# A fixed order for the first forty steps of each engine, first units in halves, filling products on TensorE

## The chip, the cores and the metric

The kernel runs on one core of a Trainium2 chip. The metric is the device time of one execution in microseconds; the kernel before takes 868.29 us (median of 3 runs, 868.08 to 869.13). Engines: PE (TensorE), ACT (ScalarE), DVE (VectorE), POOL (GpSimd), SP (issues the DMAs).

## The reference

q, k and v have 8 batches, 8 heads, 576 positions, 64 dims. Attention is within chunks of 64 positions; its output, heads laid side by side, is a matrix x of 4608 tokens by 512, which goes through a feed-forward part with weights 512 x 2048 and 2048 x 512 (given as 8-byte numbers).

```
scores = scale * q_c @ k_c.T              # per chunk of 64, scale = 1/8
attn   = exp(scores - max) / (sum + 1e-9)
x      = (attn @ v_c), heads side by side # [4608, 512]
h      = x @ w_in
g      = h * 1 / (1 + exp(-1.702 * h))
out    = g @ w_out                        # [4608, 512] float32
```

## The kernel before

Tokens are taken in 36 tiles of 128; four tiles are a block, and there are 9 blocks. The hidden dimension is cut into 16 parts of 128. One unit g (144 in all) is one block and one part: h_g is 12 matmuls of 512 columns into a PSUM bank (three products of high and low parts for each of four pieces of the model dimension, lines 634 to 636), ACT applies gelu (line 655) and copies the high part g_h (656), DVE subtracts for the low part g_l (660), and o_g_t, for each tile t of the block, adds three matmuls to that tile's output bank po_t (669 to 671). For unit 0 alone h comes in two halves of 256 columns, but in one bank, and gelu follows both.

Each of the 16 weight blocks w_j (w_in's and w_out's part j) is loaded as 8-byte words (plan_w: raw_j, two DMAs of 512 KB) and made into a high and a low part: wsc and wlow on ACT (lines 172, 176), a shift with an or on DVE (181, 182), an addition (188, called wj), wh on ACT (193), and the difference on DVE (196), after which w_j is ready. They are needed once, in the order of the units of block 0, and stay.

The first four tiles, u = 0 to 3, go through plan_first: loads of q, k, v (256 KB each), transposes of q and k on PE (266), copies to SBUF on ACT and DVE (273, 277, 279), scores on PE (289), max and subtraction on DVE (294, 295), exp on ACT (298), sum and reciprocal on DVE (302 to 305), the product with the reciprocal on POOL (308), transposes on PE (313), a copy on ACT (320), the product with v on PE (329), and x's high part on ACT (339) and low part on DVE (342). The later tiles go in pairs (plan_pair), pair 4 and pair 6 with transposes on PE (412, 480), beside block 0's units.

The order is set by class Plan: each step has an engine, a cost, a rank, the events that it needs and the buffers that it takes and gives. emit() plays the steps through with these costs and handover times, gives each free engine its ready step of the lowest rank, and writes the instructions in that order. Each engine then runs its instructions in program order and waits for what a step needs. Two buffers exist for h (bank pair hp) and for g, one output bank per tile.

Of the kernel before, what the change touches and what calls it, by code (L numbers as in the profile page):

```python
# [20 lines left out]

class Plan:
# [6 lines left out]
    HANDOVER = {None: 0.0, PE: 0.2, ACT: 0.2, DVE: 0.15, POOL: 0.15, DMA: 2.0}  # L29
    TABLE_LOAD = 1.3  # L30

    def __init__(self, buffers):
        self.free = dict(buffers)
        self.steps = []

# [3 lines left out]
    def emit(self):  # L39
# [13 lines left out]
        table, now, left = None, 0.0, len(self.steps)  # L53
        order = []
        while left:
            for e, heap in ready.items():
                while heap and busy[e] <= now + 1e-9:
                    skipped, pick = [], None
                    while heap:
                        rank, i = heapq.heappop(heap)  # L60
                        take = self.steps[i][6]
                        if all(self.free[b] >= take.count(b) for b in take):
# [15 lines left out]
                    post(now + cost + (self.HANDOVER[e] if e == DMA else 0), 0, give)  # L78
                    post(now + cost + self.HANDOVER[e], 1, make)
            assert at or not left, sorted((s[2], s[5]) for h in ready.values() for s in [self.steps[i] for _, i in h])[:9]  # L80
            now = at[0][0] if at else now
            while at and at[0][0] <= now + 1e-9:
                _, _, kind, what = heapq.heappop(at)
                if kind == 0:
                    for b in what:
                        self.free[b] += 1
                else:
                    for i in users.pop(what, ()):
# [10 lines left out]
def tile_chunk_attention_ffn(  # L99
# [14 lines left out]
    P = 128  # L114
# [22 lines left out]
    make_identity(nc, ident)  # L137

# [10 lines left out]
    def slot_user(j):  # L149

        return divmod(NF - 1 - j, 2)

    def plan_w(j):
# [23 lines left out]

        def high():
            hf, hi, li, lu = words()
            w_tmp[j] = tmp = more.tile([P, 1024], I32, tag="wtmp", name=f"wtmp_{j}")  # L180
            nc.vector.tensor_scalar(tmp, hi, 3, None, op0=ALU.logical_shift_left)
            nc.vector.scalar_tensor_tensor(
                tmp, hi, -(2**31), tmp, op0=ALU.bitwise_and, op1=ALU.bitwise_or
# [19 lines left out]
        u, kind = slot_user(j)  # L203
        need = [f"{('s', 'xp')[kind]}_{u}"] if u < TB else []
        e = lambda n: f"{n}_{j}"
        plan.add(DMA, 1.6, rank - 5.5, lambda: load(0), need=need, make=e("rawi"), take=[f"w{j}"])
        plan.add(DMA, 1.6, rank - 5.5, lambda: load(1), need=[e("rawi")], make=e("raw"))
        plan.add(ACT, 1.1, rank, scale, need=[e("raw")], make=e("wsc"))
        plan.add(ACT, 1.1, rank, low, need=[e("wsc")], make=e("wlow"))
        plan.add(DVE, 1.95, rank, high, need=[e("wsc")], make=e("whigh"), take=["tmp"])  # L210
        plan.add(DVE, 1.25, rank, join, need=[e("whigh"), e("wlow")], make=e("wj"))
        plan.add(ACT, 1.05, rank - 3.5, part_h, need=[e("wj")], make=e("wh"))
        plan.add(DVE, 1.25, rank - 2, part_l, need=[e("wh")], make=e("w"), give=["tmp"])
# [27 lines left out]
    def plan_first(u):  # L241
# [29 lines left out]

        def t_q():
            nc.scalar.activation(st["tr"][:, 0], st["ps"][0], AF.Copy)

        def t_k():
            if k_act:
                nc.scalar.activation(st["tr"][:, 1], st["ps"][1], AF.Copy)
            else:
                nc.vector.tensor_copy(st["tr"][:, 1], st["ps"][1])

        def s_pe():
            t = st["tr"]
            st["s"] = sc = ps_o.tile([P, NP, 2, CH], F32, tag=f"po{u % 2}", name=f"s_{u}")
# [7 lines left out]
        def s_max():  # L291
            sc = st["s"]
            m = two.tile([P, NP, 2], F32, tag="m", name=f"m_{u}")
            nc.vector.tensor_reduce(m, sc, axis=AX.X, op=ALU.max)
            nc.vector.tensor_tensor(st["e"], sc, bc(m), op=ALU.subtract)
# [11 lines left out]
        def s_norm():  # L307
            nc.gpsimd.tensor_tensor(st["e"], st["e"], bc(st["r"]), op=ALU.mult)  # L308

        def e_pe():  # L310
            st["ps"] = ps = ps_o.tile([P, NP, 2, CH], F32, tag=f"po{2 + u % 2}", name=f"eTp_{u}")
# [10 lines left out]
        def x_pe():  # L322
            va, et = st["v"], st["et"]
            ps = ps_a.tile([P, 2, 2, NP, CH], F32, tag="att", name=f"x_{u}")
            for n in range(NP):
                for h in range(2):
                    for c in range(2):
                        r = slice(64 * c, 64 * c + 64)
                        nc.tensor.matmul(
                            ps[64 * h : 64 * h + 64, c, 0, n, :],  # L330
                            va[r, 2 * n + h, :],
                            et[r, n, h, :],
                            start=True,
                            stop=True,
                        )
            st["x"] = ps[:, :, 0].rearrange("p c n i -> p n c i")

        def x_hi():
            nc.scalar.activation(x_part(x_h, u), st["x"], AF.Copy)

        def x_lo():
            nc.vector.tensor_tensor(x_part(x_l, u), st["x"], x_part(x_h, u).bitcast(F32), op=ALU.subtract)

        rank = u - 95
        plan.add(DMA, 2.0, u - 103, load_qk, make=ev("rows"), take=[slot(0)])
        plan.add(DMA, 1.0, u - 102.5, load_v, make=ev("v"), take=[slot(1)])
        plan.add(PE, 0.95, rank, t_pe, need=[ev("rows")], make=ev("tp"), take=["hp", "hp"])
        plan.add(ACT, 0.6, rank, t_q, need=[ev("tp")], make=ev("tq"), give=["hp"])
        plan.add(ACT if k_act else DVE, 0.68, rank, t_k, need=[ev("tp")], make=ev("tk"), give=["hp"])
        plan.add(  # L350
            PE, 1.2, rank + 0.6, s_pe, need=[ev("tq"), ev("tk"), ev("v")], make=ev("s"),
            take=[f"po{u % 2}"], give=[slot(0)],
        )
        plan.add(DVE, 1.37, rank + 0.6, s_max, need=[ev("s")], make=ev("m"), give=[f"po{u % 2}"])
        plan.add(ACT, 0.63, rank + 0.6, s_exp, need=[ev("m")], make=ev("ex"), table="exp")
        plan.add(DVE, 1.1, rank + 0.6, s_sum, need=[ev("ex")], make=ev("z"))
        plan.add(POOL, 1.07, rank + 0.6, s_norm, need=[ev("z")], make=ev("n"))
        plan.add(PE, 0.5, rank + 1.7, e_pe, need=[ev("n")], make=ev("ep"), take=[f"po{2 + u % 2}"])
        plan.add(ACT, 0.6, rank + 1.7, e_act, need=[ev("ep")], make=ev("et"), give=[f"po{2 + u % 2}"])
        plan.add(  # L360
            PE, 0.75, rank + 1.5, x_pe, need=[ev("et"), ev("v"), "xa_0"], make=ev("xp"),
            take=["att", "att"], give=[slot(1)],
        )
        plan.add(ACT, 0.6, rank + 1.5, x_hi, need=[ev("xp")], make=ev("xh"))
        plan.add(DVE, 0.69, rank + 1.5, x_lo, need=[ev("xh")], make=ev("xl"), give=["att", "att"])

# [4 lines left out]
    def plan_pair(u):  # L371
# [162 lines left out]
        if pe:  # L534
            for t in range(2):
# [9 lines left out]
                plan.add(ACT, 0.6, rank, lambda t=t: t_q(t), need=[ev(f"tp{t}")], make=ev(f"tq{t}"), give=["att"])  # L545
                plan.add(DVE, 0.68, rank, lambda t=t: t_k(t), need=[ev(f"tp{t}")], make=ev(f"tk{t}"), give=["att"])
# [225 lines left out]
```

## Time and profile before

| what | value |
|---|---|
| median of 3 runs | 868.29 us |
| the profiled execution | 868.24 us, its span 866.5 us |
| PE busy | 849.3 us (98%), 5882 matmul instructions |
| DVE busy, ACT busy, POOL busy | 392.3 us (45%), 319.1 us (37%), 32.3 us (4%) |
| mean granted clock of TensorE | 0.993 |

Read it with care: the shares are means over the whole span. The span in 40 slices has PE at 7 and 6 tenths at its two ends and 9 tenths between, DVE at 9 tenths in slices 3 and 4 and ACT at 9 in slices 2 to 4. Busy times of matmuls overlap one another.

### The profile page before, as it was taken

The numbers are of one execution on the slowest core, as the hardware profiler recorded it, in microseconds if no ns is written. First come the engines' busy times: TensorE is split into PE (matmuls) and PEld (weight loads), VectorE is DVE, ScalarE is ACT, GpSimd is POOL, SyncE is SP. The second block draws the span as 40 slices with busy tenths as digits, with TensorE's granted clock in tenths as the row PEclk, the third lists the DMA queues.
The fourth block names the chain that finished last, engine by engine and source line by source line (L and its number), as shares of the span: only waits on it lengthen the run. The fifth ranks groups of instructions, "written<-read, shape, count | busy, mean of one in ns | idle before, by whom it ended". The sixth has DMA issues, their size and how long they took to land.

```text
span 866.5 us, 14153 instructions
## 1 busy us (share of the span) xinstructions
PE 849.3 (98%) x5882; PEld 703.0 (81%) x5882; DVE 392.3 (45%) x511; ACT 319.1 (37%) x459; POOL 32.3 (4%) x24
## 2 busy tenths in 40 slices
PE   7699999999999999999999999999999999999998
PEld 5588888888888888888888888888888888888886
DVE  5899985353534252616253444445343524121111
ACT  3999652332424242324242423223241424222221
POOL 1000000000000000000000000000000000000000
PEclk9799999999999999999999999999999999999999
DMA  9997243234313022402231232113101010010001
GB/s 236 319 300 212 45 74 80 52 56 73 92 25 49 22 47 57 72 2 48 74 58 18 41 75 51 31 38 85 25 1 26 37 35 3 1 45 5 1 0 49
DMA packets 194592, 55.47 MB, mean 64 GB/s; under 512 B 179680, under 2 KB 187872, under 8 KB 194528
## 3 DMA queue, kind: packets, MB, share of 16 engines
q1 hardware_dynamic: 194528, 54.57, 27.3%
q8 instruction: 46, 0.75, 0.4%
q14 instruction: 18, 0.15, 0.1%
HBM read 45.09 MB, written 9.44 MB: 63 GB/s over the span
## 4 chain that ended last, share of the span: by engine, by line
PE 95%; SPq 2%; DMA 1%; DVE 1%; ACT 1%; issue 1%; POOL 0%; DVEq 0%; POOLq 0%; ACTq 0%
PE po L669 16%; PE po L670 15%; PE po L671 15%; PE hp L634 15%; PE hp L635 15%; PE hp L636 15%; PE s L445 2%; PE x L510 2%; SPq L231 1%; DMA raw<-in_moe_w_out_dram 1%; PE qkTp L412 0%; ACT raw L172 0%; POOL first_b L308 0%; PE eTp L480 0%; SPq L163 0%
## 5 line engine op out<-in xcount | busy, mean ns | idle before, releaser
L660 DVE TENSOR_TENSOR g_l<-hp,g_h 128x512 fp32r<-128x512 f32 x144 | 99.5, 691 | 351.2 <-ACT g_h L656 350.1
L669 PE MATMUL po<-w,g_l 128*128 128x512 f32 x576 | 226.4, 393 | 0.1
L671 PE MATMUL po<-w,g_h 128*128 128x512 f32 x576 | 224.3, 389 | 0.0
L670 PE MATMUL po<-w,g_h 128*128 128x512 f32 x576 | 224.2, 389 | 0.0
L634 PE MATMUL hp<-x_l,w 128*128 128x512 f32 x572 | 223.2, 390 | 0.0
L636 PE MATMUL hp<-x_h,w 128*128 128x512 f32 x572 | 222.7, 389 | 0.0
L635 PE MATMUL hp<-x_h,w 128*128 128x512 f32 x572 | 222.6, 389 | 0.0
L655 ACT ACTIVATE hp<-hp 128x512 f32<-128x512 f32 x144 | 83.9, 583 | 305.3 <-PE hp L636 269.6
L656 ACT ACTIVATE g_h<-hp 128x512 fp32r<-128x512 f32 x144 | 86.1, 598 | 141.3 <-PE po L671 139.6
L669 PEld LDWEIGHTS po<-w,g_l 128*128 128x128 f32 x576 | 108.1, 188 | 23.9 <-DVE g_l L660 1.0
L671 PEld LDWEIGHTS po<-w,g_h 128*128 128x128 f32 x576 | 108.1, 188 | 22.7
L670 PEld LDWEIGHTS po<-w,g_h 128*128 128x128 f32 x576 | 108.1, 188 | 21.8
L636 PEld LDWEIGHTS hp<-x_h,w 128*128 128x128 f32 x572 | 107.4, 188 | 22.8 <-DVE w L196 0.4
L634 PEld LDWEIGHTS hp<-x_l,w 128*128 128x128 f32 x572 | 107.4, 188 | 22.4 <-DVE g_l L660 0.2
L635 PEld LDWEIGHTS hp<-x_h,w 128*128 128x128 f32 x572 | 107.4, 188 | 22.0
L493 DVE STREAM_TRANSPOSE eT<-e 32x512 f32<-32x512 f32 x112 | 78.7, 703 | 29.6 <-POOL e L473 27.8
L473 POOL TENSOR_TENSOR e<-e,r 128x1024 f32<-128x1024 f32 x14 | 26.7, 1905 | 671.8 <-ACT hp L655 671.8
L427 DVE STREAM_TRANSPOSE qkT<-raw 128x1024 f32<-128x1024 f32 x28 | 34.7, 1240 | 29.4 <-PE s L445 26.8
L525 ACT ACTIVATE x_h<-x 128x512 fp32r<-128x512 f32 x32 | 17.4, 593 | 58.4 <-PE x L510 58.4
L466 DVE TENSOR_REDUCE z<-e 128x16 f32<-128x1024 f32 x16 | 19.5, 1219 | 22.2 <-ACT e L462 22.2
L528 DVE TENSOR_TENSOR x_l<-x,x_h 128x512 fp32r<-128x512 f32 x32 | 20.6, 685 | 6.7 <-ACT x_h L525 6.7
L445 PEld LDWEIGHTS s<-qkT 64*64 64x64 f32 x1024 | 18.2, 135 | 5.6 <-issue 5.3
(64 smaller groups left out, 410.5 us busy)
## 6 DMA issues: line engine op xcount, KB each, us to landing
out_dram<-ob SPq DMA_DIRECT2D x36, 256.0 KB, 2.0
raw<-in_moe_w_in_dram SPq DMA_DIRECT2D x16, 512.0 KB, 7.8
raw<-in_moe_w_out_dram SPq DMA_DIRECT2D x16, 512.0 KB, 8.3
v<-in_v_dram SPq DMA_DIRECT2D x28, 256.0 KB, 3.3
raw<-in_q_dram SPq DMA_DIRECT2D x144, 32.0 KB, 2.0
raw<-in_k_dram SPq DMA_DIRECT2D x144, 32.0 KB, 2.0
raw<-in_q_dram SPq DMA_DIRECT2D x48, 24.0 KB, 1.9
raw<-in_k_dram SPq DMA_DIRECT2D x48, 24.0 KB, 1.9
```

The source lines that it names most:

```text
L427: nc.vector.transpose(st["tr"][:, i].rearrange("p n (t j) -> p (n t) j", j=32), st["raw"][:, i].rearrange("p n t j -> p (n t) j"),)
L445: nc.tensor.matmul(o, tr[r, 0, n, cols], tr[r, 1, n, cols], start=True, stop=True)
L493: nc.vector.transpose(st["et"][po : po + 32, :, 32 * a : 32 * a + 32], st["e"][pi : pi + 32, :, 32 * b : 32 * b + 32],)
L634: nc.tensor.matmul(hp, wh, xl, start=cc == 0, stop=False)
L635: nc.tensor.matmul(hp, wh, xh, start=False, stop=False)
L636: nc.tensor.matmul(hp, wl, xh, start=False, stop=cc == NCC - 1)
L655: nc.scalar.activation(h_t[g], h_t[g], AF.Gelu_apprx_sigmoid)
L656: nc.scalar.activation(gh, h_t[g], AF.Copy)
L660: nc.vector.tensor_tensor(gl, h_t.pop(g), gh.bitcast(F32), op=ALU.subtract)
L669: nc.tensor.matmul(po, gl[:, c], w[:, 0, :], start=j == 0, stop=False)
L670: nc.tensor.matmul(po, gh[:, c], w[:, 0, :], start=False, stop=False)
L671: nc.tensor.matmul(po, gh[:, c], w[:, 1, :], start=False, stop=j == NF - 1)
```

## The change

- ORDER names the first steps of PE, ACT, DVE and of the loads, about forty of each engine and 21 loads; emit() takes them in exactly this sequence and lets no other step on an engine until its list is used up. "+n" in PE's list is n matmuls of the 128 x 128 identity with itself (float32), into a bank that nothing reads.
- The plan's handover times change, and a step that needs one of its own engine no longer waits a handover. Some costs change. Both act on the order of all later steps.
- q and k of a first tile are loaded and transposed as steps of their own, both DMAs of a weight block are one step, shift and or on DVE are two. Each first tile has its own bank for scores and for the transposes after them.
- The copy of k is on ACT for tiles 1, 2 and 3 (before: 2). The product with the reciprocal moves from POOL to DVE. For tiles 0 and 1 the low part of x no longer comes from DVE: PE computes the product with v again into a second place (xq), adds the negated identity times the high part (xs), and ACT copies it out.
- Units 0 and 1 are taken in halves of 256 columns with a bank, a gelu, a g_h and a g_l for each half; o_g_0 and o_g_1 need the first half alone.
- The table of gelu is loaded by an activation of one column (gt) behind the last exp of the first tiles.

The diff, cut to its core:

```diff
+ORDER = {
+    PE: (
+        "warm tkp_0 tqp_0 +4 s_0 tkp_1 tqp_1 tqp_2 +4 tkp_2 s_1 s_2 ep_0 +9 tqp_3 +4 xp_0 xq_0 "
+        "tkp_3 +2 xs_0 ep_1 +2 s_3 +7 xp_1 xq_1 +5 xs_1 +6 h_0_0 ep_2 ep_3 +4 xp_2 +14 o_0_0 xp_3 "
+        "o_0_1 h_1_0 h_0 h_1 o_1_0 o_0_3 o_0_2 o_1_1 h0_2 h_2 o_1_2 o_1_3 tp0_4"
+    ),
+    ACT: (
+        "tq_0 tk_1 tq_1 ex_0 tq_2 tk_2 wsc_0 ex_1 et_0 wlow_0 tq_3 xh_0 ex_2 tk_3 et_1 xl_0 wh_0 "
+        "wsc_1 xh_1 ex_3 xl_1 gt wlow_1 et_2 et_3 gh_0_0 xh_2 wh_1 wsc_2 xh_3 wlow_2 gh_1_0 gh_0 "
+        "wh_2 gh_1"
+    ),
+    DVE: (
+        "tk_0 m_0 sm_0 z_0 n_0 m_1 sm_1 m_2 sm_2 wshift_0 z_1 n_1 whigh_0 wj_0 z_2 m_3 sm_3 w_0 "
+        "n_2 z_3 n_3 wshift_1 whigh_1 wj_1 gl_0_0 xl_2 w_1 wshift_2 xl_3 whigh_2 gl_1_0 wj_2 "
+        "gl_0 w_2 gl_1"
+    ),
+    DMA: (
+        "k_0 q_0 k_1 q_1 q_2 k_2 raw_0 q_3 v_0 k_3 raw_1 v_1 raw_3 v_3 v_2 raw_2 rows0_4 raw_4 "
+        "raw_6 rows1_4 raw_5"
+    ),
+}
...
-    HANDOVER = {None: 0.0, PE: 0.2, ACT: 0.2, DVE: 0.15, POOL: 0.15, DMA: 2.0}
+    HANDOVER = {None: 0.0, PE: 0.25, ACT: 0.12, DVE: 0.12, POOL: 0.15, DMA: 2.9}
...
+                        turn = name == first[e][-1] if first.get(e) else name not in listed
+                        if turn and all(self.free[b] >= take.count(b) for b in take):
...
+    NH = 2
+    K_ACT, X_ACT = (1, 2, 3), (0, 1)
...
+    minus = const.tile([P, P], F32R, tag="minus", name="minus")
+    nc.vector.tensor_scalar(minus, ident, -1.0, None, op0=ALU.mult)
...
         def s_norm():
-            nc.gpsimd.tensor_tensor(st["e"], st["e"], bc(st["r"]), op=ALU.mult)
+            nc.vector.tensor_tensor(st["e"], st["e"], bc(st["r"]), op=ALU.mult)
...
+        def x_sub():
+            for c in range(2):
+                nc.tensor.matmul(
+                    st["xps"][:, c, 1], minus, x_part(x_h, u)[:, :, c], start=False, stop=True
+                )
+
+        def x_low():
+            if x_act:
+                nc.scalar.activation(x_part(x_l, u), x_ps(1), AF.Copy)
+            else:
+                nc.vector.tensor_tensor(
+                    x_part(x_l, u), x_ps(0), x_part(x_h, u).bitcast(F32), op=ALU.subtract
+                )
...
+                if u in K_ACT:
+                    plan.add(ACT, 1.08, rank, lambda t=t: t_qk(t), need=[ev(f"tp{t}")], make=ev(f"tq{t}"), give=["att", "att"])
...
+        if g < NH:
+            for i in range(2):
+                m = ("_0", "")[i]
+                plan.add(
+                    PE, 1.42, g - 0.2, lambda i=i: h_half(i),
+                    need=[f"w_{j}", f"xl_{2 * i}", f"xl_{2 * i + 1}"] + [ev("h") + "_0"] * i + ([f"h_{g - 1}{m}"] if g else []),
+                    make=ev("h") + m, take=["hp"],
+                )
...
+    def keep_warm(count, bank="po3"):
+        if bank not in warm:
+            warm[bank] = ps_o.tile([P, P], F32, tag=bank, name=f"warm_{bank}")
+        for _ in range(count):
+            nc.tensor.matmul(warm[bank], ident, ident, start=True, stop=True)
...
+    plan.add(ACT, 0.2, -80, gelu_table, make="gt", need=[f"ex_{TB - 1}"], table="gelu")
+    for e, names in ORDER.items():
+        names = names.split()
+        for i, name in enumerate(names):
+            if name[0] == "+":
+                bank = "po0" if "xp_0" in names[:i] else "po3"
+                names[i] = f"keep_{i}"
+                plan.add(PE, 0.11 * int(name), -1000, lambda n=int(name), b=bank: keep_warm(n, b), make=names[i])
+        plan.first[e] = " ".join(names)
```

Names of steps: tqp, tkp are the transposes of q, k; tq, tk their copies; s scores; m, sm max and subtraction; ex exp; z sum and reciprocal; n the product with it; ep, et the transposes and their copy; xp the product with v; xh, xl x's two parts; gh, gl those of g, with "_0" behind the unit for a first half; wshift, whigh, wj, w DVE's four steps for a weight block; rows0_4, tp0_4 the first load and transposes of pair 4.

## Rows read from the trace of the kernel before

**Rows 1.** The page's chain that ended last, shares of the span by engine

```profile
PE 95%; SPq 2%; DMA 1%; DVE 1%; ACT 1%; issue 1%; POOL 0%; DVEq 0%; POOLq 0%; ACTq 0%
```

**Rows 2.** Windows: window, length, busy us of PE, PEld, DVE, ACT, POOL; clock, DMA, GB/s

```profile
12.00:16.00 4.00, 3.01 (x76) 2.46 (x73) 2.43 (x6) 2.79 (x5) 1.38 (x2) 1.00 1.35 220
...
24.00:28.00 4.00, 1.13 (x32) 0.94 (x32) 3.83 (x7) 3.78 (x6) 0.93 (x1) 0.64 1.07 379
...
32.00:36.00 4.00, 4.00 (x21) 4.00 (x22) 3.75 (x5) 4.00 (x5) 0.00 (x0) 0.58 1.01 174
...
68.00:72.00 4.00, 4.00 (x24) 3.37 (x23) 4.00 (x5) 4.00 (x5) 0.00 (x0) 1.00 1.10 325
```

**Rows 3.** Timeline of PE: start us, us, instructions, and idle time before

```profile
1.36 3.35 PE L725 MATMUL warm<-ident 128*128 128x128 f32 x14 [1.36 <-POOL ident masks.py:199]
...
6.81 1.15 PE L289 MATMUL s<-first_a 64*64 64x64 f32 x32 [0.88 <-DVE first_a L279]
7.89 0.65 PE L266 MATMUL qkTp<-ident,first_a 128*128 128x128 f32 x4
...
14.43 0.69 PE L329 MATMUL x<-first_b 64*64 64x64 f32 x32 [0.84 <-ACT first_b L320]
14.94 1.12 PE L289 MATMUL s<-first_a 64*64 64x64 f32 x32
...
31.84 0.58 PE L647 MATMUL hp<-x_l,w 128*128 128x256 f32 x1
...
36.37 0.40 PE L634 MATMUL hp<-x_l,w 128*128 128x512 f32 x1
...
47.72 0.39 PE L634 MATMUL hp<-x_l,w 128*128 128x512 f32 x1
```

**Rows 4.** The chain that ended last in order of time: start us, us, what

```profile
45.64 0.87 PE qkTp L412 x8
...
75.75 0.23 PE hp L634
...
77.11 0.49 PE po L669
```

**Rows 5.** Timeline of DVE, the steps of weights and what follows them

```profile
23.86 0.69 DVE L181 TENSOR_SCALAR wtmp<-raw 128x1024 int32<-128x1024 int32 x1 [2.16 <-ACT raw L172]
24.59 1.23 DVE L182 SCALAR_TENSOR_TENSOR wtmp<-raw,wtmp 128x1024 int32<-128x1024 int32 x1
25.73 0.68 DVE L302 TENSOR_REDUCE z<-first_b 128x8 f32<-128x512 f32 x1
...
31.78 1.22 DVE L188 CUSTOM_DVE_ANT_0 wtmp<-raw,wtmp 128x2048 uint16<-128x2048 uint16 x1
32.91 0.68 DVE L342 TENSOR_TENSOR x_l<-x,x_h 128x512 fp32r<-128x512 f32 x1
...
41.55 1.22 DVE L188 CUSTOM_DVE_ANT_0 wtmp<-raw,wtmp 128x2048 uint16<-128x2048 uint16 x1
42.84 0.69 DVE L660 TENSOR_TENSOR g_l<-hp,g_h 128x512 fp32r<-128x512 f32 x1
43.45 0.68 DVE L422 COPY qkT<-qkTp 128x512 f32<-128x512 f32 x1
...
74.11 1.22 DVE L196 TENSOR_TENSOR w<-wtmp,w 128x1024 fp32r<-128x1024 f32 x1
```

**Rows 6.** Timeline of ACT

```profile
15.19 0.60 ACT L339 ACTIVATE x_h<-x 128x512 fp32r<-128x512 f32 x1 [0.33 <-PE x L329]
...
36.72 1.28 ACT L655 ACT_TABLE_LOAD   x1
...
72.36 1.99 ACT L193 ACTIVATE w<-wtmp 128x1024 fp32r<-128x1024 f32 x2
```

**Rows 7.** Timeline of SP, and the issue with its size and time to landing

```profile
12.20 1.14 SPq L231 DMA_DIRECT2D first_b<-in_v_dram  x1
...
first_b<-in_v_dram SPq DMA_DIRECT2D x1, 256.0 KB, 6.1
```

More of the change, by code (lines that the diff above doesn't have):

```diff
@@ L52, in emit @@
         busy = {e: 0.0 for e in self.HANDOVER}
-        table, now, left = None, 0.0, len(self.steps)
+        first = {e: names.split()[::-1] for e, names in self.first.items()}
+        listed = {name for names in first.values() for name in names}
+        table, now, left = "exp", 0.0, len(self.steps)
         order = []
@@ L87, in emit @@
                 else:
-                    for i in users.pop(what, ()):
+                    ev, engine, same = what
+                    for i in users.get(ev, ()):
+                        if (self.steps[i][0] == engine and engine != DMA) != same:
+                            continue
                         waits[i] -= 1
@@ L201, in part_l @@
             )
-        u, kind = slot_user(j)
-        need = [f"{('s', 'xp')[kind]}_{u}"] if u < TB else []
+        need = [slot_user(j)] if slot_user(j) else []
         e = lambda n: f"{n}_{j}"
[L206 to L213, printed above, removed]
+        plan.add(DMA, 2.85, rank - 5.5, load, need=need, make=e("raw"), take=[f"w{j}"])
+        plan.add(ACT, 1.08, rank, scale, need=[e("raw")], make=e("wsc"))
+        plan.add(ACT, 1.08, rank, low, need=[e("wsc")], make=e("wlow"))
+        plan.add(DVE, 0.71, rank, shift, need=[e("wsc")], make=e("wshift"), take=["tmp"])
+        plan.add(DVE, 1.2, rank, high, need=[e("wshift")], make=e("whigh"))
+        plan.add(DVE, 1.17, rank, join, need=[e("whigh"), e("wlow")], make=e("wj"))
+        plan.add(ACT, 1.02, rank - 3.5, part_h, need=[e("wj")], make=e("wh"))
+        plan.add(DVE, 1.17, rank - 2, part_l, need=[e("wh")], make=e("w"), give=["tmp"])
     x_h, x_l = {}, {}
@@ L349, in plan_first @@
-        plan.add(ACT if k_act else DVE, 0.68, rank, t_k, need=[ev("tp")], make=ev("tk"), give=["hp"])
+            nc.scalar.activation(x_part(x_h, u), x_ps(0), AF.Copy)
+        def x_sub():
[9 more added lines that the diff above has]
+                    x_part(x_l, u), x_ps(0), x_part(x_h, u).bitcast(F32), op=ALU.subtract
+                )
@@ new lines, in plan_first @@
+        rank = u - 95
+        plan.add(DMA, 1.2, u - 103, lambda: load(0), make=ev("q"), take=[slot(0)])
+        plan.add(DMA, 1.2, u - 102.9, lambda: load(1), make=ev("k"))
+        plan.add(DMA, 1.2, u - 101.5, load_v, make=ev("v"), take=[slot(1)])
+        plan.add(PE, 0.45, rank, lambda: t_pe(0), need=[ev("q")], make=ev("tqp"), take=["hp"])
+        plan.add(PE, 0.45, rank, lambda: t_pe(1), need=[ev("k")], make=ev("tkp"), take=["hp"])
+        plan.add(ACT, 0.55, rank, t_q, need=[ev("tqp")], make=ev("tq"), give=["hp"])
@@ new lines, in plan_first @@
+        plan.add(ACT if k_act else DVE, 0.62, rank, t_k, need=[ev("tkp")], make=ev("tk"), give=["hp"])
+        plan.add(PE, 0.95, rank + 0.6, s_pe, need=[ev("tq"), ev("tk")], make=ev("s"), take=[f"po{u}"], give=[slot(0)])
+        plan.add(DVE, 0.71, rank + 0.6, s_max, need=[ev("s")], make=ev("m"))
+        plan.add(DVE, 0.64, rank + 0.6, s_sub, need=[ev("m")], make=ev("sm"), give=[f"po{u}"])
+        plan.add(ACT, 0.55, rank + 0.6, s_exp, need=[ev("sm")], make=ev("ex"), table="exp")
+        plan.add(DVE, 1.12, rank + 0.6, s_sum, need=[ev("ex")], make=ev("z"))
@@ L350, in plan_first @@
+        plan.add(DVE, 0.64, rank + 0.6, s_norm, need=[ev("z")], make=ev("n"))
+        plan.add(PE, 0.45, rank + 1.7, e_pe, need=[ev("n")], make=ev("ep"), take=[f"po{u}"])
+        plan.add(ACT, 0.55, rank + 1.7, e_act, need=[ev("ep")], make=ev("et"), give=[f"po{u}"])
         plan.add(
-            PE, 1.2, rank + 0.6, s_pe, need=[ev("tq"), ev("tk"), ev("v")], make=ev("s"),
-            take=[f"po{u % 2}"], give=[slot(0)],
-        )
-        plan.add(DVE, 1.37, rank + 0.6, s_max, need=[ev("s")], make=ev("m"), give=[f"po{u % 2}"])
@@ L355, in plan_first @@
[L355 to L363, printed above, removed]
@@ L691, in plan_ffn @@
         last = ["x"] if j == NF - 1 else []
-        if g == 0:
-            plan.add(
-                PE, 1.37, g - 0.2, lambda: h_half(0), need=[need[0], "xl_0", "xl_1"], make=ev("h0"), take=["hp"]
-            )
-            plan.add(PE, 1.37, g - 0.2, lambda: h_half(1), need=[ev("h0"), "xl_2", "xl_3"], make=ev("h"))
+        if g < NH:
[5 more added lines that the diff above has]
+                    make=ev("h") + m, take=["hp"],
+                )
+                plan.add(
+                    ACT, 0.7, g - 5, lambda i=i: g_hi(i), need=[ev("h") + m] + [ev("gh") + "_0"] * i,
+                    make=ev("gh") + m, take=[] if i else ["g"], table="gelu",
+                )
+                plan.add(DVE, 0.4, g - 5, lambda i=i: g_lo(i), need=[ev("gh") + m], make=ev("gl") + m, give=["hp"])
         else:
@@ L699, in plan_ffn @@
             plan.add(PE, 1.37, g - 0.2, lambda: h_pe(1), need=[ev("h0")], make=ev("h"), give=last)
-        plan.add(ACT, 1.18, g - 5, g_hi, need=[ev("h")], make=ev("gh"), take=["g"], table="gelu")
-        plan.add(DVE, 0.69, g - 5, g_lo, need=[ev("gh")], make=ev("gl"), give=["hp"])
+            plan.add(ACT, 1.18, g - 5, g_hi, need=[ev("h")], make=ev("gh"), take=["g"], table="gelu")
+            plan.add(DVE, 0.69, g - 5, g_lo, need=[ev("gh")], make=ev("gl"), give=["hp"])
         for t in range(TB):
```

167 lines of the change are left out of this document (90 added, 77 removed).

## The prediction

> **What bounds the kernel now.** I read the chain that ended last first: PE holds 95% of it [rows 1]. The reader should ask next where the other 5% lie, and the windows answer: from 12 to 16 us PE is busy 3.01 of 4.00 us, from 24 to 28 us 1.13, from 32 us on it is full in every window I read [rows 2]. So a change of the opening is worth the time by which it brings the later, full PE forward, if that PE stays full. The PE timeline dates it: the first product of the feed-forward part starts at 31.84 us, and its unit (24 matmuls, 256 columns each) lasts to 36.37, 4.53 us, because the granted clock there is 0.58, partly the 1.2 GHz level [rows 2, 3]; at the 2.4 GHz level 24 halves of the 0.23 us that a 512-column matmul takes in the chain [rows 4] are 2.8 us. Up to 5.5 us of start and 1.7 us of clock look free.
>
> The second bound shows only when the other engines are read in the same windows: from 68 to 72 us DVE is busy 4.00 and ACT 4.00 of 4.00, with PE full as well [rows 2]. They turn the sixteen weight blocks w_0 to w_15 from 8-byte words into two parts, and PE lives from hand to mouth: w_7's last step on DVE runs from 74.11 to 75.33 [rows 5], the first product with it stands in the chain at 75.75, and at 77.11 PE waits (0.49 instead of 0.23) for g_l of unit 6, with no output product left over [rows 4]. The slack there is 0.4 us. After it PE never waits until the end, so the time of the changed kernel is that of before plus the shift of this point, and PE's lead at an earlier time counts only if DVE's is as large.
>
> **Part by part, PE first.** Up to the first scores nothing moves: k comes ahead of q, but both are needed; the products run 6.81 to 7.89 [rows 3], and the first "+4" of filling lies in the wait before them. After it come t_k and t_q of tile 1 (0.45 each, half of the 0.87 us for eight [rows 4]), and tqp_2 must wait for a PSUM buffer that ACT empties (transposes end 0.65 after their start [rows 3], copy 0.60 [rows 6]): 7.89 + 0.65 + 0.60, about 9.2 us.
>
> From there PE's queue is a list, and I add it up to xp_3, the point that holds the others back. Four transpose steps and four ep at 0.45: 3.6. Three score steps at 1.08 (6.81 to 7.89 [rows 3]): 3.2. Five x steps (xp_0, xq_0, xp_1, xq_1, xp_2) at 0.51 (14.43 to 14.94 [rows 3]): 2.6. Two subtractions on PE, two 256-column matmuls each, unseen in the trace: at least 0.23, at most the 0.69 of an x step; I take 0.3, as they have the width of the half matmuls: 0.6. h_0_0, 12 half matmuls: 1.4. o_0_0, three at 0.23: 0.7. Together 12.1 us.
>
> Then the filling: 57 products after tqp_2 (4+9+4+2+2+7+5+6+4+14). What is one worth? In the opening 7 products are 14 instructions in 3.35 us, 0.24 each [rows 3], twice the 0.109 of a transpose of the same width later (0.87 / 8 [rows 4]): that is the lower clock level. At the upper level a product of two instructions is 0.22 us. The change's own plan counts 0.11 for a product, one instruction's worth. Bounds 0.11 and 0.24; I take 0.218, the nearest row twice: 12.4 us.
>
> The Trainium skill weighs in here: "TensorE: Matmul & The Clock Gate", section "Back-to-back issue gap", gives 128-column matmuls in a stream with weight loads about 81 ns each. The trace doesn't agree for this four-byte type: it has 109 ns. By the page a filling product is an estimated 0.16 us, the filling 9.2 us, and with the steps below the whole 2.0 us faster than before (866.2) where I forecast a small loss; that result lies inside the first rival.
>
> So xp_3 starts at 9.2 + 12.1 + 12.4 = 33.7 us, and h_0_0 at 26.3, 5.5 us before 31.84. Is PE held up by anything else? v_1 is the last input of h_0_0. Before, the twelfth 256 KB load was issued at 12.20 and landed 6.1 us later, 18.3 [rows 7]. Two such loads fewer (1.19 us each at 220 GB/s) and two weight blocks more (1.05 MB, 2.8 us each at 379 GB/s [rows 2]) give 21.4, while xp_1 reaches the head of PE's queue at 22.6. The block raw_0 lands at 18.3 - 6 x 1.19 + 2.8 = 13.9 instead of with the twelve loads before it; w_0, six conversion steps of 0.7 to 1.2 us later, is ready before 26.3. Past v_3 and v_2, which now stand behind raw_1 and raw_3 on SP, the same count gives v_2 at 26.7 (twelve small loads, three blocks), before xp_2's turn at 29.4; no load of the list waits for a buffer, and POOL keeps nothing of this stage. With the queue full, the clock stays at its upper level: it read 1.00 from 12 to 16 us with PE at 3.01 of 4.00 [rows 2].
>
> After xp_3 (call it S): x 0.5, o_0_1 0.7, three half units 4.2, four o 2.7, unit 2 2.7, two o 1.4: S + 12.2 = 45.9 us with three h units, eight o and no transposes of pair 4. Before, PE had three h units, five o and two transpose steps at 47.72 [rows 3]; three o more and 2 x 0.87 off make 48.0. PE's lead: 2.1 us.
>
> **Then DVE.** Its list goes as fast as PE lets it: xl_3 stands ahead of whigh_2, wj_2 and w_2, and needs xp_3, which the filling before o_0_0 ("+14", 3.1 us) delays; behind the waiting xl_3 stands all weight work. xh_3 ends at S + 1.4 (x 0.69 [rows 3], ACT 0.60 [rows 6]); xl_3 0.61 (as 42.84 to 43.45), whigh_2 1.14 (24.59 to 25.73 [rows 5]): S + 3.1. gl_1_0 waits for two half passes on ACT behind h_1_0 (unseen; each between 0.15 and 0.60, I take 0.37): it ends at about S + 3.95. wj_2 1.13 (31.78 to 32.91 [rows 5]), then ACT's wh_2 1.0 (two in 1.99 [rows 6]) with handovers of 0.15, in which gl_0 is hidden, w_2 1.13, gl_1 0.36: S + 7.75 = 41.5 us. Before, gl_1 was done at 43.45, but DVE had then also done the first three steps of w_3, whose third started at 41.55 [rows 5]: 0.73 + 1.14 + 1.13 = 3.0 us. On the same work the change is at 41.5 + 3.0 + 0.2 (first wait for ACT's wsc_3) = 44.7 against 43.45: DVE is 1.2 us late while PE is 2.1 us early. ACT is no better off, with two k copies and two x_l more and four short passes for two long ones.
>
> The edits that trade work come out even on DVE: k copies of tiles 1 and 3 and x_l of tiles 0 and 1 leave it (four of 0.6), four n steps come from POOL (four of 0.6). The negated identity costs 0.2 us while DVE has no input. The gelu table now loads beside PE's filling; without that cover its 1.28 us [rows 6] would lie before the first g, as it did. The ScalarE copy for pairs is never reached: their u is 4 or 6, and the list of tiles is 1 to 3. New handover times reorder the remaining steps: w_7's ACT step is first of two from 72.36 [rows 6], ended by 73.4, and its DVE step starts only at 74.11, so an order can be 0.7 us better, up to 1.9 if a whole shift and high stand elsewhere, or as much worse; I take 0.
>
> **The sum.** DVE saturated from there, w_7 comes at 75.33 + 1.2, PE starts it 0.4 us less late: +0.8 us. The profiled execution took 868.24 (span 866.5 and 1.7 around it), the median is 868.29: 869.0 us.
>
> **Rivals.** First, faster: the filling is cheaper than two transposes. At 0.11 it is 6.3 us, and waits take PE's place: v_1 at 21.4, x 0.7, ACT 0.6, subtraction 0.3, ACT 0.6, handovers 0.4: h_0_0 at 24.0; behind that last ACT pass the table load 1.3, a weight pass 1.0 (two in 1.99) and a copy 0.6 lead to xp_2 at 27.0, and x 0.5, 14 x 0.11 and o_0_0 0.7 to xp_3 near 30. DVE's list ends at 37.75, and 37.75 + 3.2 - 43.45 - 0.4 = -2.9: 865.3. For it speaks the plan's own cost; against it that every 128-wide instruction in the trace has 0.109 or more. Note that even then DVE gives back half of PE's lead. Second, slower: the two vector engines are the bound from the list on and fall further back. With filling at 0.24 (S = 35.0) and each half pass on ACT at 0.60, the list ends at 43.3, and 43.3 + 3.2 - 43.45 - 0.4 = +2.65: 870.9. It decides the sign from a list end of about 42.7, where w_7 is 2.1 us late. For it speaks the full ACT [rows 2]; against it that PE's order may slip pair 4's steps behind. Third, the change doesn't do what it says: in a fixed list a step that is late holds up all behind it, and an engine that waits so early (ACT for raw_0 with wsc_0, ahead of ex_1) passes it on until the earlier start is lost; PE then follows the weights as before, within 1.7 us on either side.
>
> **How the numbers follow.** A difference under 0.2% (1.74 us) can't be told from none. Forecast and third case, 866.5 to 870.0: 0.47. First rival, with orders that finish w_7 sooner: 0.28 faster. Second: 0.25 slower. The likeliest case alone spans 867.2 to 870.0; bounds of the filling and of the order widen it to 865.0 to 871.3.
>
> **What would show it.** Right: h_0_0 near 26.3 at a granted clock of 1.00; filling instructions of 0.11; xp_3 near 33.7; gl_1 near 41.5; afterwards PE waiting for w_5 to w_7 or g_l. Wrong: filling products of 0.11, PE waiting for v_1 before xp_1, or a w_7 before 75 us with no PE wait between 50 and 80 us, which would let the lead of PE stand.

## Result and profile after

The changed kernel takes 869.94 us (median of 15 runs, 869.72 to 871.16), the kernel before 868.23 in the same comparison (15 runs, 867.66 to 869.21): ratio 1.0021, interval 1.0013 to 1.0029. It is 1.7 us slower: a small difference, but the interval doesn't reach 1. The forecast was 869.0 with a range of 865.0 to 871.3.

The profiled execution took 869.94 us too, its span 868.1 (before 868.24 and 866.5). The page's first and fourth parts, busy time and the chain that ended last:

```profile
PE 862.0 (99%) x6084; PEld 716.8 (83%) x6084; DVE 392.7 (45%) x514; ACT 322.4 (37%) x468; POOL 27.4 (3%) x20
...
PE 94%; DVE 4%; ACT 1%; issue 1%; POOL 0%; POOLq 0%; ACTq 0%
```

PE's share of the chain went down by one point [rows 1], and DVE's up from 1% to 4%. (In the 40 slices of the page before, PE's 7 and 6 tenths are the first two, its last slice has 8, and DVE has 9 in slices 3 to 5: the hole lies at the start alone.) The windows, with the columns of [rows 2], say where PE is short of work:

```profile
12.00:16.00 4.00, 4.00 (x71) 3.93 (x68) 3.66 (x7) 2.83 (x4) 0.00 (x0) 1.00 1.21 224
24.00:28.00 4.00, 4.00 (x64) 3.93 (x54) 3.03 (x7) 3.07 (x5) 0.00 (x0) 1.00 0.95 284
...
32.00:36.00 4.00, 3.94 (x58) 3.32 (x56) 2.36 (x3) 1.82 (x2) 0.00 (x0) 1.00 1.07 378
48.00:52.00 4.00, 3.63 (x21) 2.89 (x20) 4.00 (x5) 3.92 (x6) 0.00 (x0) 1.00 1.05 378
68.00:72.00 4.00, 3.89 (x21) 3.00 (x20) 3.93 (x6) 3.96 (x6) 0.00 (x0) 1.00 0.94 321
108.00:112.00 4.00, 3.83 (x19) 2.93 (x19) 3.90 (x7) 2.12 (x4) 0.00 (x0) 1.00 0.29 47
```

The hole of the opening is closed, and the clock reads 1.00 in all these windows (before 0.64 from 24 us and 0.58 from 32 us on [rows 2]). But from 32 to 36 us DVE, busy 3.75 of 4.00 us before [rows 2], is busy 2.36, and PE has gaps at 48, 68 and 108 us. PE's timeline of the stretch that decides (L810 is filling, L717 to L719 a half unit, L359 ep, L376 x, L742 an output product, L477 and L548 transposes of a pair, L706 a whole unit):

```profile
25.82 1.50 PE L810 MATMUL warm_po<-ident 128*128 128x128 f32 x12
27.08 0.36 PE L717 MATMUL hp<-x_l,w 128*128 128x256 f32 x1
...
28.59 1.04 PE L359 MATMUL eTp<-ident,first_b 128*128 128x128 f32 x8
29.46 1.06 PE L810 MATMUL warm_po<-ident 128*128 128x128 f32 x8
30.45 0.69 PE L376 MATMUL x<-first_b 64*64 64x64 f32 x32
31.07 3.39 PE L810 MATMUL warm_po<-ident 128*128 128x128 f32 x28
34.52 0.50 PE L742 MATMUL po<-w,g_l 128*128 128x512 f32 x1
...
35.43 0.69 PE L376 MATMUL x<-first_b 64*64 64x64 f32 x32
...
48.14 1.03 PE L477 MATMUL qkTp<-ident,rows 128*128 128x128 f32 x8
49.55 0.50 PE L742 MATMUL po<-w,g_l 128*128 128x512 f32 x1 [0.37 <-DVE g_l L733]
...
111.54 1.06 PE L548 MATMUL eTp<-ident,e 128*128 128x128 f32 x8 [0.17 <-DVE e L541]
...
153.49 0.50 PE L706 MATMUL hp<-x_l,w 128*128 128x512 f32 x1
```

Unit 0 starts at 27.08 instead of 31.84 [rows 3], and from there to 49 us PE is never idle. Yet between unit 0's first half (ended 28.59) and the next h product, unit 1's at 36.85, stand 18 filling products, 4.4 us (29.46 to 30.45 and 31.07 to 34.52). PE's ledger from 31.84 on: start 4.8 earlier, unit 0's halves at the full clock 1.6 saved; against that 4.4 of filling and 2.1 of ep and x steps that before stood ahead of unit 0. Sum: nothing won. PE comes to its list's last step, the transposes of pair 4, at 48.14, where before the same work would have ended at 48.0.

DVE's timeline shows the other half. L400 is x_l, L223 whigh, L237 the last step of a weight block, L733 g_l:

```profile
33.93 0.69 DVE L219 TENSOR_SCALAR wtmp<-raw 128x1024 int32<-128x1024 int32 x1
36.82 0.69 DVE L400 TENSOR_TENSOR x_l<-x,x_h 128x512 fp32r<-128x512 f32 x1 [2.21 <-ACT x_h L387]
37.43 1.22 DVE L223 SCALAR_TENSOR_TENSOR wtmp<-raw,wtmp 128x1024 int32<-128x1024 int32 x1
...
41.98 1.23 DVE L237 TENSOR_TENSOR w<-wtmp,w 128x1024 fp32r<-128x1024 f32 x1 [0.79 <-ACT w L234]
43.13 0.42 DVE L733 TENSOR_TENSOR g_l<-hp,g_h 128x256 fp32r<-128x256 f32 x1
...
45.80 1.23 DVE L229 CUSTOM_DVE_ANT_0 wtmp<-raw,wtmp 128x2048 uint16<-128x2048 uint16 x1
```

DVE stands 2.21 us at the head of its list, before xl_3, with weight work queued behind. Its list ends at 43.55; the third step of w_3 ends at 46.94, where before this much was done at 43.45 [rows 5]: 3.5 us late. Then DVE and ACT run nearly full, and the chain in order of time shows how it reaches PE:

```profile
66.67 1.14 DVE z L534
...
68.33 1.23 DVE e L541
69.56 1.15 DVE w L237
70.71 0.04 issue
70.75 0.50 PE hp L708
```

The softmax of pair 4 (z, e) runs just ahead of the last step of w_6, and PE starts the first product that reads this step's result, the third of unit 6, at 70.75 instead of 70.47, when the one before it was through. The same happens for g_l at 49.55 (some 0.6 us late), behind the next softmax at 111.5 (0.3) and at 153.5 (0.4), where an h product (L706) needs the bank that g_l frees: with 0.4 for w_6, taking in the 0.1 that a matmul behind a wait is longer, 1.7 us. Before, one such wait cost 0.25, at 77.1 [rows 4]. So 0.1 from the list and 1.45 from the waits make the 1.6 by which the span grew.

### The profile page after: what moved, and what is told of

It reads as the page before. It is cut to its first block, busy times and chain, and to the rows that moved or that the text cites. A ratio compares the mean times of both kernels' runs of the same rounds, so it can differ in the third digit from the quotient of the medians.

```text
span 868.1 us, 14549 instructions
## 1 busy us (share of the span) xinstructions
PE 862.0 (99%) x6084; PEld 716.8 (83%) x6084; DVE 392.7 (45%) x514; ACT 322.4 (37%) x468; POOL 27.4 (3%) x20
## 4 chain that ended last, share of the span: by engine, by line
PE 94%; DVE 4%; ACT 1%; issue 1%; POOL 0%; POOLq 0%; ACTq 0%
PE po L742 15%; PE po L744 14%; PE po L743 14%; PE hp L706 14%; PE hp L708 14%; PE hp L707 14%; PE warm_po L810 2%; PE x L578 2%; PE s L513 2%; DVE w L237 1%; DVE wtmp L223 1%; DVE wtmp L229 1%; PE s L331 0%; PE qkTp L310 0%; DVE g_l L733 0%
## 5 line engine op out<-in xcount | busy, mean ns | idle before, releaser
L733 DVE TENSOR_TENSOR g_l<-hp,g_h 128x512 fp32r<-128x512 f32 (+1 forms) x146 | 99.8, 684 | 346.1 <-ACT g_h L728 345.2
L742 PE MATMUL po<-w,g_l 128*128 128x512 f32 x576 | 226.4, 393 | 0.4 <-DVE g_l L733 0.4
L706 PE MATMUL hp<-x_l,w 128*128 128x512 f32 x568 | 221.7, 390 | 0.1
L727 ACT ACTIVATE hp<-hp 128x512 f32<-128x512 f32 (+1 forms) x146 | 84.4, 578 | 229.7 <-PE hp L708 228.3
L728 ACT ACTIVATE g_h<-hp 128x512 fp32r<-128x512 f32 (+1 forms) x146 | 86.6, 593 | 208.8 <-PE po L744 207.8
L742 PEld LDWEIGHTS po<-w,g_l 128*128 128x128 f32 x576 | 108.1, 188 | 23.8 <-DVE g_l L733 0.6
L744 PEld LDWEIGHTS po<-w,g_h 128*128 128x128 f32 x576 | 108.1, 188 | 22.7
L743 PEld LDWEIGHTS po<-w,g_h 128*128 128x128 f32 x576 | 108.2, 188 | 21.8
L706 PEld LDWEIGHTS hp<-x_l,w 128*128 128x128 f32 x568 | 106.6, 188 | 22.4 <-DVE g_l L733 0.5
```

What stands on the lines that cost most here:

```text
L706: nc.tensor.matmul(hp, wh, xl, start=cc == 0, stop=False)
L727: nc.scalar.activation(hp, hp, AF.Gelu_apprx_sigmoid)
L728: nc.scalar.activation(g_t[g][0][:, c], hp, AF.Copy)
L733: nc.vector.tensor_tensor(gl[:, c], hp, gh[:, c].bitcast(F32), op=ALU.subtract)
L742: nc.tensor.matmul(po, gl[:, c], w[:, 0, :], start=j == 0, stop=False)
L743: nc.tensor.matmul(po, gh[:, c], w[:, 0, :], start=False, stop=False)
```

## Experiments

Three theories were put against each other. T: filling costs what its instructions cost (0.235 us a product); it holds up PE's queue and, through xl_3, DVE's list. O: the new handover times and the order that they give behind the lists cost the time. C: the filling is needed for the clock, and without it more is lost than gained. The kernel before stood at 868.39 to 868.49 us beside these runs and at 868.23 beside the change, so a difference between a run and the change's 869.94 is good to some 0.3 us. Ratios are against the kernel before.

**Half the filling.** Plan and order as in the change, half the products issued:

```diff
-lambda n=int(name), b=bank: keep_warm(n, b)
+lambda n=int(name) // 2, b=bank: keep_warm(n, b)
```

> The changed kernel with every count of filling products halved (29 of 57 behind tqp_2 are left out; order and plan are the same). Theory T, filling too long, then DVE's weights: in the changed kernel's trace a filling product takes 0.235 us, so PE gains up to 6.6 us up to xp_3, less what then waits for v_1: xp_3 near 30 instead of 35.4, DVE's list ends near 38.5 instead of 43.55, the time falls by 3.5 to 5 us to 865 to 866.5. Rival O, the order behind the list is the cause: 869 to 870. Rival C, the filling holds the clock: with half of it the granted clock falls before unit 0, and 868 to 870 comes out.

866.09 us (7 runs, 865.80 to 867.61), ratio 0.9971 [0.9961, 0.9982]: 3.85 us below the change and faster than both. The profile is of its longest execution. PE's timeline, and a window with the columns of [rows 2]:

```profile
29.21 1.83 PE L810 MATMUL warm_po<-ident 128*128 128x128 f32 x14
...
31.99 0.69 PE L376 MATMUL x<-first_b 64*64 64x64 f32 x32
```

```profile
20.00:24.00 4.00, 3.03 (x96) 2.74 (x92) 3.85 (x7) 2.85 (x4) 0.00 (x0) 1.00 1.02 327
```

xp_3 came 3.44 us sooner (31.99 against 35.43), gl_1 3.43 sooner (39.70 against 43.13), w_6's last step 3.42 sooner (66.06 against 69.48): the shift of DVE's list goes through to the weights unchanged, as T says, though xp_3 and the list's end (40.12) came 2.0 and 1.6 us later than T expected. PE is now idle a quarter of the time from 20 to 24 us, and the clock still reads 1.00. What PE waits for (line waited with, releaser, total us, times, longest):

```profile
PE qkTp L477 <- DMA rows<-in_q_dram: 1.1, 1, 1.1
PE x L376 <- DMA first_b<-in_v_dram: 1.0, 1, 1.0
PE x L376 <- ACT raw L214: 0.9, 1, 0.9
```

32 products fewer (30 of them behind tqp_2, not the 29 of the expectation) are 7.5 us, but only 3.4 came through: waits took the place of part of the rest, above all two for v. The third line is xp_0's, which doesn't read what L214 writes; the copy that it reads was done at 15.42, and v_0, issued at 8.45, landed 7.9 us later, at 16.35, just before xp_0 at 16.52. The first line, at 67 us, is the wait for pair 6's rows: up to it units 2 to 5 start 3.4 us sooner than in the change, unit 6 1.85, and those from 14 on 2.3 sooner.

**No filling.**

```diff
+        if not count:
+            return
...
+lambda n=0, b=bank: keep_warm(n, b)
```

> The changed kernel with no filling at all (order and plan the same). T: PE waits for v_1 and for ACT, h_0_0 near 23.5, xp_3 near 29.5 to 30; if the clock stays at 1.00, 865 to 866.5, much as with half. C: the granted clock falls to 0.5 in the waits before unit 0, which costs 1.5 us or more against the run with half the filling. O: 869 to 870.

867.04 us (11 runs), 0.9984 [0.9975, 0.9992]. Windows:

```profile
20.00:24.00 4.00, 1.97 (x92) 1.72 (x88) 3.76 (x8) 3.36 (x6) 0.00 (x0) 1.00 1.17 320
24.00:28.00 4.00, 3.21 (x14) 2.91 (x15) 3.86 (x8) 3.74 (x6) 0.00 (x0) 0.54 0.89 283
28.00:32.00 4.00, 3.23 (x43) 2.71 (x43) 2.92 (x4) 2.50 (x6) 0.00 (x0) 0.60 1.19 271
```

PE was busy 1.97 of 4.00 us, in the last of these not at all, and then the clock read 0.54: the 1.2 GHz level. Unit 0's halves took 0.21 us a matmul (0.12 with filling), xp_3 came at 32.76, later than with half the filling. Without filling C is right, by about 1 us (it expected 1.5 or more, and the two runs' intervals overlap slightly); with half of it C is wrong. The eleven executions bear this out: the four with a mean clock of 0.998 to 1.000 took 865.73 to 866.55 us, the seven at 0.995 or 0.996 took 866.78 to 869.50. The Trainium skill ("TensorE: Matmul & The Clock Gate", section "What's actually happening") has the lower level as the default that activity releases; these rows agree.

**Only the filling before o_0_0 cut,** from 14 products to 3:

```diff
+lambda n=3 if name == "+14" else int(name), b=bank: keep_warm(n, b)
```

> Only the 14 filling products ahead of o_0_0 are cut to 3. T: o_0_0 starts 2.6 us earlier (31.9), with it xp_3, xl_3 and DVE's list end (near 41.0), and the time falls by 2 to 2.6 us: 867.3 to 868. O and C: within 0.5 us of the changed kernel, 869.5 to 870.

867.84 us (11 runs, 867.54 to 868.12), 0.9993 [0.9985, 1.0002]: 2.1 us less than the change. xp_3 starts at 33.39, DVE's wait before xl_3 is gone (it starts at 34.96, straight behind wshift_2), and each unit from 2 to 143 starts 2.02 to 2.09 us sooner than in the change. One early shift, kept to the end: T.

**The new planner alone.** The kernel before with the changed handover times, DMAs' included, and no list:

```diff
-    HANDOVER = {None: 0.0, PE: 0.2, ACT: 0.2, DVE: 0.15, POOL: 0.15, DMA: 2.0}
+    HANDOVER = {None: 0.0, PE: 0.25, ACT: 0.12, DVE: 0.12, POOL: 0.15, DMA: 2.9}
...
-                    post(now + cost + self.HANDOVER[e], 1, make)
+                    post(now + cost, 1, (make, e, True))
+                    post(now + cost + self.HANDOVER[e], 1, (make, e, False))
```

> The kernel before with the changed class Plan alone (handover times, no handover on the step's own engine, exp table loaded at the start), no list, no filling, no other edit. T: the opening is that of before, 867.5 to 868.9. O: the new handover times give a worse order of the later steps, 869.3 to 870.5.

870.53 us (6 runs), 1.0031 [1.0019, 1.0042]. T missed the time and O's number fits, but not its place. SP's timeline, and ACT's first step of raw_0:

```profile
14.69 2.16 SPq L174 DMA_DIRECT2D raw<-in_moe_w_in_dram  x3
16.90 1.79 SPq L179 DMA_DIRECT2D raw<-in_moe_w_out_dram  x3
```

```profile
25.02 1.10 ACT L183 ACTIVATE raw<-raw 128x1024 f32<-128x1024 f32 x1 [5.89 <-DMA raw<-in_moe_w_out_dram]
```

With the new rules the plan issues three first halves of blocks before a second half (two before), raw_0 is whole at 25.0 (before 22.7), and unit 0 starts at 34.78. The loss is in the opening: unit 2 starts 2.6 us later than before, the last units 2.2. In the change both DMAs of a block are one step, so this can't occur there; the next run asks directly.

**The change with the old handover times.**

```diff
-    HANDOVER = {None: 0.0, PE: 0.25, ACT: 0.12, DVE: 0.12, POOL: 0.15, DMA: 2.9}
+    HANDOVER = {None: 0.0, PE: 0.2, ACT: 0.2, DVE: 0.15, POOL: 0.15, DMA: 2.0}
```

> The changed kernel with the handover times of before (the listed first steps stay, the order behind the lists differs). T: the loss is made before the lists end, so 869 to 870.5, as the changed kernel. O: the new handover times cost some 2 us behind the list, as the run with the new rules alone might be read: 867.5 to 868.5.

869.94 us (11 runs), 1.0020 [1.0011, 1.0029], the change's own number. O falls as far as the handover times go; the changed costs, and that a step waits no handover for one of its own engine, were not run by themselves.

**Less weight work on DVE.** For w_3 to w_15 the and-or step that completes the high part is left out (the shift takes its turn), 1.2 us less on DVE for each block.

```diff
+            if j >= 3:
+                nc.vector.tensor_scalar(w_tmp[j], hi, 3, None, op0=ALU.logical_shift_left)
+                return
```

> The changed kernel without DVE's and-or step (one pass over 128x1024, 1.14 us) for the weight blocks w_3 to w_15, so those weights are wrong; order, filling and all else are the same. T: PE's waits for DVE behind the list (0.4 at 49.5, 0.5 at 70.7, 0.6 at 111 us) go, and nothing more, as the filling stays: 868.0 to 868.7, 1.2 to 1.9 us less. If DVE is not late at all: 869.7 to 870.1.

869.19 us (11 runs), 1.0011 [1.0002, 1.0020]: 0.75 less than the change, half of what T expected. The chain in order of time shows why:

```profile
56.19 6.82 DMA raw<-in_moe_w_out_dram
...
63.03 1.14 ACT raw L210
...
64.19 1.28 ACT L534
...
65.48 1.07 ACT e L534
...
69.55 1.15 DVE w L241
```

w_6 comes at the same 70.7, now behind a block's landing, ACT's step on it, the load of exp's table and exp (the opening of this execution was also 0.4 us later, xp_3 at 35.86). In this chain the waits after the lists are a bound of DVE, ACT and the blocks' landing together, not of DVE alone, so thinning one frees little.

**The kernel before with a warm PE.** 20 filling products in the waits of PE before unit 0, nothing else:

```diff
+            if u >= 2:
+                fill({2: 12, 3: 2}[u])
...
+            if u == 3:
+                fill(6)
```

> The kernel before with 20 filling products put only where PE waited in its opening (12 ahead of x of tile 2, 6 ahead of the transposes of tile 3, 2 ahead of x of tile 3). The clock then stays at 1.00 and unit 0 takes 2.8 us instead of 4.5. T: DVE's w_1 to w_7 come when they came before, and the slack at w_7 is 0.25 to 0.4 us, so the time falls by no more than 0.5 us: 867.8 to 868.5. If PE's lead counts by itself: 866.7 to 867.0, 1.7 us less.

867.96 us (11 runs), 0.9997 [0.9988, 1.0005]: 0.4 us less than before at most, and the last units start 0.3 sooner, though the clock was 1.00 and unit 0's matmuls 0.12 us apart. PE's waits after 26 us:

```profile
PE hp L648 <- DVE w L196: 0.8, 1, 0.8
...
PE hp L661 <- DVE w L196: 0.5, 1, 0.5
PE hp L659 <- DVE x_l L354: 0.3, 1, 0.3
```

A faster PE alone turns into waits for weights and x_l. Of unit 0's clock, 1.7 us in the prediction, 0.3 to 0.4 came through.

**Half the filling, pair 6's rows loaded sooner,** against the wait of 1.1 us:

```diff
-                    DMA, 2.0, rank - 3,
+                    DMA, 2.0, rank - (6 if u == 6 else 3),
```

> The run with half the filling, and the row loads of pair 6 two weight blocks earlier on SP. There PE waited 1.1 us at 67 us for those rows. T: this wait goes; DVE then binds at the next point: 865.0 to 865.8, 0.3 to 1.0 us less than with half the filling. If the earlier rows put the weight blocks off: 866 to 867.

866.56 us (11 runs, 865.63 to 868.93), 0.9982 [0.9973, 0.9991]. The wait is gone from the profiled execution (865.82): xp_3 starts 4.08 us sooner than in the change (31.35), and every unit from 2 to 143 4.04 to 4.11 sooner, as T says. But the median isn't below that of half the filling, so what the edit is worth stays open.

**Filling only where PE would wait,** 18 products:

```diff
+lambda n={3: 2, 15: 4, 24: 3, 27: 4, 29: 2, 35: 3}.get(i, 0), b=bank: keep_warm(n, b)
```

> The changed kernel (order and plan the same) with filling only where the run with none showed PE waiting, and no longer than those waits at 0.235 us each: 2 ahead of s_0, 4 ahead of xp_0, 3 of xp_1, 4 of xs_1, 2 of h_0_0, 3 of o_0_0, 18 in place of 61. T: the clock holds at 1.00, h_0_0 near 25.2, xp_3 near 31.5 (32.0 with half the filling), 865.3 to 866.5, the fastest of the variants or level with half. C: less filling than half is too little, the granted clock falls before unit 0 as with none, xp_3 near 32.8: 866.5 to 868.

867.62 us (11 runs, 866.23 to 871.02), 0.9996 [0.9987, 1.0006]. The best execution has xp_3 at 30.47, the earliest of all and 4.96 us before the change's. Units 2 to 5 keep that lead (4.94 to 4.97), then the wait for pair 6's rows stands there again:

```profile
PE qkTp L477 <- DMA rows<-in_q_dram: 1.4, 1, 1.4
```

The later units start 3.7 us sooner. Other executions lie up to 4.8 us above this one: the five with a mean clock of 1.000 took 866.23 to 867.11 us, the six at 0.997 to 0.999 took 867.62 to 871.02. Missed by T; C's number fits, and the lower clock of the slower six points to its cause.

**Half the filling ahead of h_0_0, all of it behind.**

```diff
+lambda n=int(name) // 2 if i < 30 else int(name), b=bank: keep_warm(n, b)
```

> The changed kernel with the filling ahead of h_0_0 halved and that behind it (4 and 14) whole. T, PE's queue in front and DVE's list behind it, by the ledger: h_0_0 1.3 us earlier as with half (25.75), o_0_0 and xp_3 1.3 earlier, 868.4 to 868.9, so that this gain and that of the single cut ahead of o_0_0 (2.1) add up to nearly the 3.85 of half the filling. If only the filling ahead of o_0_0 matters, since DVE waits for xp_3 alone: 869.5 to 870.

867.91 us (11 runs), 0.9996 [0.9987, 1.0004]: 2.0 less than the change, more than the 1.0 to 1.5 that T expected. h_0_0 at 25.05, xp_3 at 33.42, gl_1 at 41.13: 2.0 each, and units 2 to 143 1.95 to 2.05.

**Half ahead, and 4 products instead of 14 before o_0_0.**

```diff
+lambda n=4 if name == "+14" else int(name) // 2, b=bank: keep_warm(n, b)
```

> Half the filling everywhere and 4 products (not 7) ahead of o_0_0, 26 in all. T: the two single gains (2.1 from the cut ahead of o_0_0, 2.0 from half ahead of h_0_0) add up, 865.3 to 866.3, 0 to 0.7 us less than with half the filling, and the fastest kernel of this study. If the vector engines' supply already binds with half the filling: the same as half, 865.9 to 866.6. If the clock needs more filling: above 866.6 with a wide spread, as with filling cut to the waits.

867.54 us (9 runs, 865.58 to 870.98), 0.9990 [0.9977, 1.0004]. Three executions reach 865.6 to 865.9, the median doesn't: the two parts add up only at best. In the profiled one (867.97) xp_3 comes at 31.33, 4.1 us sooner than in the change, but PE then waits 0.9 for x_l and 1.0 for pair 6's rows, and 2.0 is left.

## Why the prediction was nearly right

The result lies at the upper end of the likeliest case's own range (867.2 to 870.0). The ratio, 1.0021, is just past the 0.2% that the prediction took for no difference; the two medians are just within. That the number came within 1 us is partly luck: two errors of opposite sign met, as the steps show.

- **Start of unit 0, 26.3.** It was 27.08, at clock 1.00, and no load held PE up, as forecast; v_1, issued at 14.59, landed 7.2 us later, at 21.8 (forecast 21.4), before xp_1 at 23.27. ACT's timeline has the first step of raw_0 (landing forecast for 13.9) and, below, the x_h of tile 3 that DVE's xl_3 waits for.

```profile
13.16 1.15 ACT L210 ACTIVATE raw<-raw 128x1024 f32<-128x1024 f32 x1 [1.21 <-DMA raw<-in_moe_w_out_dram]
...
36.19 0.60 ACT L387 ACTIVATE x_h<-x 128x512 fp32r<-128x512 f32 x1 [2.37 <-PE x L376]
```

- **Filling, 0.218 us a product.** From the start of each of the ten stretches to the next instruction the 57 products take 13.4 us, 0.235 each: 1.0 more than the 12.4 of the sum. The first rival, the plan's 0.11, is out. The Trainium skill's 81 ns for a 128-column matmul in a stream ("TensorE: Matmul & The Clock Gate", "Back-to-back issue gap") doesn't hold for these float32 products either: the trace has about 118 ns an instruction.
- **xp_3 at 33.7.** It started at 35.43. Beside the filling, small steps were a little longer: an x step by itself 0.62 instead of 0.51, a half unit 1.51 instead of 1.4, o_0_0 0.91 instead of 0.7.
- **List end of DVE 41.5, 1.2 us late.** 43.55 and 3.5 us late on the same work, 2.3 later than forecast: 1.7 from xp_3, 0.4 between xp_3 and the end (the terms as the prediction gives them add up to S + 7.87, 0.1 more than its 7.75), the rest in w_3. The mechanism (weight work queued behind a waiting xl_3) is the one forecast; the cuts of filling, which move xp_3, gl_1 and the time together, show it.
- **PE's lead, 2.1 us.** It was none (48.14 against 48.0): xp_3's 1.7 and another 0.5 behind it.
- **Slack at w_7, order at 0.** This is the step that failed. w_7's last step came at 74.21 (before 74.11), so the order made good nearly all of the 3.5 us; but w_6's came at 69.48 instead of 68.84, behind pair 4's softmax, and w_6 was the block that PE waited for. The rest of the loss came through g_l and pair 6's softmax, where the sum had nothing. The slack of 0.4 was also counted to unit 7's first product (75.75 [rows 4]); the last step makes the low part, which only the third of each three products reads, in the same chain of before:

```profile
76.20 0.23 PE hp L636
```

  So it was 0.87. With a list end of 43.55 the prediction's own sum would have given 871.1, with 3.5 us of lateness 871.3; 869.94 came. The second rival had the list's end nearly right (43.3) and its price too high (2.65): order and slack gave back 1 us of it. (Its border, a list end of 42.7 where w_7 is 2.1 us late, is 42.35 by its own sum.)
- **Third rival.** Its outcome is close to what came (PE's lead lost, the time within 1.7 us), its cause isn't: ACT did wait 1.21 us for raw_0, but what spent the lead was PE's own filling. With half the filling, PE does wait for loads, 1.9 us for v in two steps.

So the mechanism was right as far as DVE's list: the filling holds up xp_3, and xp_3 the weight work. Its terms xp_3, list end and PE's lead were each 1.7 to 2.2 us too good. The last link, through w_7 alone with the order at 0, was wrong, and its error gave part of the others back. That the changed order of later steps costs nothing by itself is shown only for the handover times. The waits at 49, 111 and 153 us aren't taken away by an earlier list: they stand in the profiles with less filling too, and move with the list.

## What to carry to other kernels

Price what keeps an engine's clock up by the instructions issued: a float32 product here is two instructions, and in a strict queue each of them delays all that the other engines wait for behind it. Look for the least filling that still holds the clock, by its spread over many runs as well as its best time: half had the lowest median here, none and a third did not, though their best executions (865.73 and 866.23) came near half's (865.80). When the fed engine's gap closes, ask at once what feeds it; here 4.8 us of earlier start were worth nothing until DVE's list moved with it.

## What the runs showed of the hardware

The opening varies from execution to execution. In the profiled execution of the run with the old handover times (871.27, its median is 869.94) the second filling stretch stands so:

```profile
6.27 1.62 PE L810 MATMUL warm_po<-ident 128*128 128x128 f32 x8
```

In the change's profile they stand so:

```profile
5.92 1.06 PE L810 MATMUL warm_po<-ident 128*128 128x128 f32 x8
```

From the same start at 1.36 us the instructions came down from 0.24 us each later in the one than in the other; what follows was 0.9 us later up to 12 us, xp_3 1.6. Another difference stays open: in four profiles (old handover times, rows sooner, half ahead, 26 products) an x step stands still for 0.2 to 0.8 us with nothing shown that it waits for.

The profile's clock column doesn't show the lower level at the start. It reads 1.00 from 0 us in these profiles, while the first 14 filling instructions take 0.24 us each [rows 3]. Without filling, the transposes at 9 us still take 0.20 each, against 0.109 later [rows 4], in a window that reads 1.00 (the window, then PE's timeline):

```profile
8.00:12.00 4.00, 3.88 (x38) 3.29 (x34) 1.38 (x2) 1.66 (x4) 0.00 (x0) 1.00 1.14 317
```

```profile
9.01 3.24 PE L310 MATMUL qkTp<-ident,first_a 128*128 128x128 f32 x16
```

So the length of an instruction has to be read beside the column.

The change's 15 executions spread over 1.4 us, 11 with half the filling (and rows sooner) over 3.3, 11 with none over 3.8, 11 with 18 products over 4.8 and 9 with 26 over 5.4: the full filling was the steadier one, though not in step with the count.

From 20 to 24 us, with transposes, scores and small float32 products, PE was busy 3.03 of 4.00 us with half the filling, and the next window of that profile still reads 1.00. Without filling it was busy 1.97 and idle at the end, and the next two windows read 0.54 and 0.60.
